# Sigmoid attention with mixture of depths: score units on other PSUM banks, one transpose a step earlier, and a last product in two halves

## The chip, the cores and the metric

The kernel runs on one core of one Trainium2 chip. The metric is the device time of one execution in microseconds (us), the median of several runs. Everything is float32.

## The reference

Two stages, the second fed by the first. The attention has no softmax: each score goes through a sigmoid of its own. Then, for each of the 8 batches, a gate picks 128 of the 448 tokens, and only those go through a two-layer network and are changed.

```python
# q, k, v: (8 batches, 12 heads, 448 tokens, 64)
scores = matmul(q, k^T) / sqrt(64) - log(448)
attn_out = matmul(sigmoid(scores), v)                  # (8, 12, 448, 64)
x = attn_out.transpose(0, 2, 1, 3).reshape(8, 448, 768)

scores = einsum('bsd,d->bs', x, w_gate)                # one gate score per token
out = x.copy()
for b in range(8):
    top_idx = argpartition(-scores[b], 128)[:128]      # the 128 tokens with the best scores
    xe = x[b, top_idx]
    ye = maximum(xe @ w1, 0) @ w2                      # w1: 768 x 1024, w2: 1024 x 768
    out[b, top_idx] = x[b, top_idx] + sigmoid(scores[b, top_idx])[:, None] * ye
```

## The kernel before: the parts concerned

The attention runs in 12 **steps** (s = 0 to 11), each for 8 heads. A step has 7 **units** (n = 0 to 6). A unit computes scores on TensorE into two PSUM tiles of two banks each, and ScalarE then takes each tile through the sigmoid into SBUF. `values` multiplies these with V; it comes in four parts, the first after the last unit of the step itself, the other three after units 0, 1 and 2 of the next step. So after units 3, 4 and 5 there is room on TensorE for the second stage: that is the table `WORK`.

All 8 PSUM banks are in use: the ring `psc` has two tiles, and the tiles `o0` and `o1` are single. Each tile has two banks. Tiles are given out again as soon as their last reader is done, so the reader decides when the next writer may start.

```python
def banks(which):
    if which == "any":                     # turn about: psc, o, psc, o ...
        turns[1] ^= 1
        which = "psc" if turns[1] else "o"
    if which == "psc":
        return ps_sc.tile([P, 2, 512], F32, name="psc")        # bufs=2
    if which == "o":
        turns[0] ^= 1                      # turn about: o0, o1
        which = turns[0]
    return ps_o[which].tile([P, 2, 512], F32, name=f"o{which}")  # bufs=1 each

def unit(s, n):
    if (s == 0 and n in (1, 3, 5)) or (s in (1, 2, 3) and n == NF + 1):   # NF = 3
        psc = [banks(0), banks(1)]
    else:
        psc = [banks("psc"), banks("psc")]
    ...                                    # 16 matmuls; heads 0, 1 into the first tile, 2, 3 into the second
    for pr in range(2):
        ...
        nc.scalar.activation(a, psc[pr][:, :, :S], AF.Sigmoid, bias=bias_s, scale=QK_SCALE)

def keep_busy(s):
    open_outs(s)                           # o0 and o1 for the coming values
    for _ in range(4):
        nc.tensor.matmul(outs[s][0][:, 0, :HP * TT], iden,
                         wg_b.rearrange("p h t -> p (h t)"), start=True, stop=True)
```

The result of `keep_busy` is used by nothing. When the fourth part of `values` is done, `take` moves `o0` and `o1` into the tokens-by-features layout with four VectorE transposes; then `gates` (multiply by the gate vector, add up) and `gate` (the scores of a whole batch, small operations, and a write to DRAM) follow on VectorE. `turn` is VectorE's transposing of q and k for a coming step. `ranking` finds each token's place among the scores (8 large VectorE operations and their followers), `choose` turns this into indices with small matmuls, and `fetch` has the chosen rows gathered from DRAM.

The second stage treats two batches at a time, a pair p. `("t", b)` is `turn_rows(b)`, which transposes the gathered rows of batch b on TensorE. The two layers are each done with 7 products in place of 8 blocks, from sums and differences of the blocks: `(1, p, key)` is a product of the first layer, `(2, p, key)` of the second, key 1 to 7.

```python
def turn_rows(b, where="o"):
    ...                                    # 6 transposes on TensorE into one tile
    if not odd:
        nc.scalar.activation(x[:, 0:2, :, :n], ps[:, :, :KH, :n], AF.Copy)
    else:
        nc.scalar.activation(x[:, 2, :, :n], ps[:, 0, :KH, :n], AF.Copy)
        nc.vector.tensor_copy(x[:, 3, :, :n], ps[:, 1, :KH, :n])
    ...
    for dst, y, z in ((4, 2, 0), (5, 3, 4), (2, 3, 2)):        # only after the odd batch
        nc.vector.tensor_tensor(out=x[:, dst, :, :n], in0=x[:, y, :, :n],
                                in1=x[:, z, :, :n], op=ALU.subtract)
    ...

ROWS1 = {1: 0, 2: 1, 3: 3, 4: 1, 5: 4, 6: 5, 7: 2}   # which x a product of the first layer reads
# after a product: key 1: ScalarE copy.  key 2: VectorE add, ScalarE relu.  key 6: VectorE add. ...
QUARTERS = {1: ((0, 0), (0, 1), (1, 0), (1, 1)), 2: ((0, 0),), 3: ((0, 1),), 4: ((1, 0),), ...}
# second layer: one VectorE operation per quarter adds the product to the gathered rows

WORK = {
    ...
    (7, 3): [(2, 0, 3)], (7, 4): [(2, 0, 6)], (7, 5): [(2, 0, 7), ("t", 2)],
    (8, 3): [("t", 3), (1, 1, 1)], (8, 4): [(1, 1, 2), (1, 1, 6)],
    ...
    (10, 3): [(2, 1, 3)], (10, 4): [(2, 1, 5), (2, 1, 6)], (10, 5): [(2, 1, 7)],
    (11, 3): [("t", 4)], (11, 4): [("t", 5), (1, 2, 1)], (11, 5): [(1, 2, 2)],
}
```

After step 11 comes `rest`: the last three parts of `values`, then all that is left of pairs 2 and 3. Work is issued in the order of the text, and each engine takes its instructions in this order.

```python
def rest():
    for n in range(3):
        gap(NS, n)                         # the last parts of values
    ...
    shared = banks("any")
    chosen = choose(b - 1, shared[:, 1])   # b = 7, p = 2
    work = [((1, p, 6), first(p, 6, ps=shared[:, 0])),
            ((1, p, 7), begin((1, p, 7), "any"))]
    gates(2 * NS - 1)
    fetch(*chosen)
    ...
    gate(waiting.pop())                    # the scores of batch 7
    spread(b, nc.sync)                     # and their way back from DRAM to all partitions
    ...
    for item, args in work:
        finish(item, args)
    for key in (4, 5):
        do((1, p, key), "any")
    first_sums(*begin((1, p, 3), "any"), sums_too=(5, 6))
    work = {key: begin((2, p, key), "any") for key in (2, 1, 4)}
    ranking(b)
    tile5 = banks("any")
    work[5] = second(p, 5, ps=tile5[:, 0])
    chosen = choose(b, tile5[:, 1])
    second_sums(*work[2])
    hidden_sum(p, 7)
    work[6] = begin((2, p, 6), "any")
    fetch(*chosen)
    second_sums(*work[1])
    ...
    for key in (1, 2, 6, 5, 3, 7, 4):      # pair 3, second layer: the end of the kernel
        do((2, p, key), "any")
```

Of the kernel before, what the change touches and what calls it, by code (L numbers as in the profile page):

```python
# [12 lines left out]
ALU = mybir.AluOpType  # L13
# [4 lines left out]
def kernel(  # L18
# [18 lines left out]
    TT = 32  # L37
# [251 lines left out]
    def unit(s, n):  # L289


        if (s == 0 and n in (1, 3, 5)) or (s in (1, 2, 3) and n == NF + 1):
            psc = [banks(0), banks(1)]
        else:
            psc = [banks("psc"), banks("psc")]
        if n == NF:
            parts = [(x, HK) for x in range(2)]
        else:
            x, c = divmod(n, NF + 1)
            parts = [(x, 4 * c), (x, 4 * c + 2)]  # L300
        for e in range(2):
            for y, (x, r) in enumerate(parts):
                for h in range(4):
                    d = slice(h * TT, (h + 1) * TT)
                    nc.tensor.matmul(  # L305
                        psc[h // 2][y * Dh:(y + 1) * Dh, h % 2, :S],
                        kT[2 * s + x][d, e, r:r + 2, :].rearrange("d r t -> d (r t)"),
                        qT[2 * s + x][d, e].rearrange("d r t -> d (r t)"),
                        start=(e == 0), stop=(e == 1))
        for pr in range(2):  # L310
            a = attn_tile(pr, f"d{s % 2}{n}" if n < 3 else f"u{n}")
            attn[s, pr, n] = a
            nc.scalar.activation(a, psc[pr][:, :, :S], AF.Sigmoid, bias=bias_s, scale=QK_SCALE)  # L313
# [3 lines left out]
    def open_outs(s):  # L317
        if s not in outs:
            outs[s] = [banks(0), banks(1)]

    def keep_busy(s):


        open_outs(s)
        for _ in range(4):
            nc.tensor.matmul(outs[s][0][:, 0, :HP * TT], iden,  # L326
                             wg_b.rearrange("p h t -> p (h t)"), start=True, stop=True)

    def values(s, n):

# [286 lines left out]
    def second_sums(p, key, ps):  # L617
        n = CAP
        left = pairs[p].setdefault("left", [6, 8])
        for x, m in QUARTERS[key]:  # L620
# [7 lines left out]
            if not left[x]:  # L628
                scatter(b)

    def scatter(b):
        n = CAP
        nc.gpsimd.indirect_dma_start(
# [19 lines left out]
    }  # L653

    LENT = {5: [(1, 6), (1, 7), (1, 5)], 6: [(1, 3), (2, 4), (2, 5)], 7: [(2, 6), (2, 7)],
# [63 lines left out]
    def gap(s, n):  # L719
# [23 lines left out]
        if n == 3 and s > 0 and not turned_next(s) and s != LATE:  # L743
            if waiting:
                gate(waiting.pop())
            gates(2 * s - 1)
            if waiting:
                gate(waiting.pop())

    def rest():  # L750
# [5 lines left out]
        for key, slot in (((2, 6), "d10"), ((2, 7), "d11")):  # L756
            lend(*key, slot)
        shared = banks("any")
        chosen = choose(b - 1, shared[:, 1])
        work = [((1, p, 6), first(p, 6, ps=shared[:, 0])),  # L760
                ((1, p, 7), begin((1, p, 7), "any"))]
        gates(2 * NS - 1)
        fetch(*chosen)

# [3 lines left out]
        store(b, (2, 3))  # L768
        for item, args in work:
            finish(item, args)  # L770
        for key in (4, 5):
            do((1, p, key), "any")
        first_sums(*begin((1, p, 3), "any"), sums_too=(5, 6))
        work = {key: begin((2, p, key), "any") for key in (2, 1, 4)}
        ranking(b)
        tile5 = banks("any")
        work[5] = second(p, 5, ps=tile5[:, 0])
        chosen = choose(b, tile5[:, 1])
        second_sums(*work[2])
        hidden_sum(p, 7)  # L780
        work[6] = begin((2, p, 6), "any")
        fetch(*chosen)
        second_sums(*work[1])
        hidden_sum(p, 3)
        work[7] = begin((2, p, 7), "any")
        for key in (4, 5, 6, 7):
# [11 lines left out]
            do((1, p, key), "any")  # L798
        for m in (5, 6, 7, 3):
            hidden_sum(p, m)  # L800
        for key in (1, 2, 6, 5, 3, 7, 4):
            do((2, p, key), "any")

    def stream():
        for b in range(B):
            routed(b)
        put(LATE, NU - 1.5, gates, 2 * LATE - 1)
        load(0)
        load(1)
        load(2)  # L810
# [9 lines left out]
        for s in range(NS):  # L820
            for n in range(NU):
# [9 lines left out]
                        for key in ((1, 3), (2, 4)):  # L831
                            lend(*key, "raw")
                gap(s, n)
                if n == NU - 2 and s in (1, 2, 3):
                    keep_busy(s)
                if n == NU - 2:
                    turn(2 * s + 2)
                    load(2 * s + 4)
# [43 lines left out]
```

## Time and profile before

| what | value |
|---|---|
| time, median of 3 runs | 457.12 us (456.84 to 457.91) |
| span of the profiled execution | 453.4 us |
| mean granted TensorE clock | 0.996 of full speed |
| scores: TensorE, into `psc` | 148.2 us busy, 2496 records, 540 ns each |
| scores: ScalarE, one sigmoid of 128x896 | 1.00 us each, 168 of them |
| `keep_busy` on TensorE | 4.7 us busy, 24 records |
| one product of the first layer, on the chain | 2.68 us |
| one product of the second layer, on the chain | 2.58 us |

Many of TensorE's records overlap, since matmuls on 32 rows run beside each other. So the length of one record says little. What counts is how far the chain of waits moves on while a group runs: a unit takes 1.50 us there when nothing holds it. A float32 matmul shows as two records.

### The profile page before, as it was taken

To read this page: it belongs to the slowest core of one execution; us is meant where nothing else is said; L and a number is where in the kernel's file an instruction comes from. 1 tells how busy PE (TensorE), PEld (TensorE's weight loads), DVE (VectorE), ACT (ScalarE), POOL (GpSimd) and SP (SyncE) were. 2 spreads that over 40 slices of the span, in tenths; PEclk is the share of its full clock that TensorE was granted. 3 is DMA by queue.
4 is the path that set the end of the run, shared out by engine and by line. 5 is a ranking of instruction groups with operands and counts; after the bars stand their busy time and mean duration, and the time that the engine had idled before them with its cause. 6 is when DMAs were issued, how large, how long until landed. Compare 5 with 4: busy or idle time off the path is not lost.

```text
span 453.4 us, 14452 instructions
## 1 busy us (share of the span) xinstructions
PE 442.0 (97%) x6398; PEld 267.0 (59%) x6398; DVE 303.8 (67%) x663; ACT 181.8 (40%) x237; POOL 32.5 (7%) x55
## 2 busy tenths in 40 slices
PE   8999999999999999999999999999999989999994
PEld 3474745565745845554445855654454639769952
DVE  4308679993844797887634697897742849994472
ACT  3856464555555254335444345334345520101100
POOL 7000000010000100000100000010010000001001
PEclk9999999999999999999999999999999999999998
DMA  8898898999866995995566883994833999811001
GB/s 279 214 329 193 329 342 187 267 205 319 175 201 220 139 234 192 170 233 186 117 235 174 132 222 142 193 196 159 241 106 101 259 189 267 147 37 71 1 0 69
DMA packets 128334, 84.67 MB, mean 187 GB/s; under 512 B 97600, under 2 KB 112064, under 8 KB 128272
## 3 DMA queue, kind: packets, MB, share of 16 engines
q1 hardware_dynamic: 126288, 75.84, 65.1%
q0 software_dynamic: 1984, 7.91, 5.7%
q8 instruction: 50, 0.82, 0.8%
q14 instruction: 12, 0.10, 0.1%
HBM read 63.28 MB, written 20.46 MB: 185 GB/s over the span
## 4 chain that ended last, share of the span: by engine, by line
PE 93%; DVE 3%; issue 1%; ACT 1%; DMA 1%; POOLq 0%; DVEq 0%; ACTq 0%
PE o L353 28%; PE psc L305 27%; PE o L548 13%; PE o L613 12%; PE psc L548 4%; PE psc L613 3%; PE o L305 3%; PE o L818 1%; PE o L326 1%; DVE x_b L368 1%; DMA out_dram<-xe,idx 1%; ACT attn_u L313 1%; DVE gate_p L379 1%; DVE scr L376 1%; PE o L467 0%
## 5 line engine op out<-in xcount | busy, mean ns | idle before, releaser
L305 PE MATMUL psc<-qT,kT 32*64 32x448 f32 x2496 | 148.2, 540 | 0.9 <-ACT attn_u L313 0.9
L313 ACT ACTIVATE attn_u<-psc,bias_s 128x896 f32<-128x896 f32 x86 | 81.9, 1004 | 84.4 <-PE psc L305 84.3
L353 PE MATMUL o<-attn_d,raw_v 32*64 32x448 f32 x960 | 104.5, 535 | 0.4 <-ACT o L356 0.4
L353 PE MATMUL o<-attn_u,raw_v 32*64 32x448 f32 x960 | 102.2, 535 | 0.8 <-ACT o L356 0.8
L305 PEld LDWEIGHTS psc<-qT,kT 32*64 32x64 f32 x2496 | 60.2, 131 | 59.1 <-issue 40.3
L313 ACT ACTIVATE attn_d<-psc,bias_s 128x896 f32<-128x896 f32 x70 | 66.7, 1003 | 46.5 <-PE psc L305 46.4
L368 DVE STREAM_TRANSPOSE x_b<-o 128x448 f32<-128x448 f32 x48 | 26.9, 618 | 66.6 <-PE o L353 59.3
L353 PEld LDWEIGHTS o<-attn_u,raw_v 32*64 32x64 f32 x960 | 41.2, 132 | 24.9 <-issue 19.9
L353 PEld LDWEIGHTS o<-attn_d,raw_v 32*64 32x64 f32 x960 | 40.4, 132 | 19.9 <-issue 17.3
L548 PEld LDWEIGHTS o<-rows_t,w_sb 128*128 128x128 f32 x264 | 30.4, 192 | 4.5 <-issue 1.4
L548 PEld LDWEIGHTS o<-rows_t,attn_d 128*128 128x128 f32 x264 | 30.3, 192 | 3.9 <-DVE scr L376 1.4
L548 PE MATMUL o<-rows_t,w_sb 128*128 128x128 f32 x264 | 31.9, 278 | 0.4 <-DVE rows_t L515 0.3
L548 PE MATMUL o<-rows_t,attn_d 128*128 128x128 f32 x264 | 31.6, 277 | 0.3 <-DVE rows_t L521 0.3
L379 DVE TENSOR_REDUCE gate_p<-scr 128x14 f32<-128x448 f32 x48 | 29.8, 622 | 1.7
L376 DVE TENSOR_TENSOR scr<-x_b,wg_b 128x448 f32<-128x448 f32 x48 | 29.6, 616 | 1.0
L624 DVE SCALAR_TENSOR_TENSOR xe<-o,gate,xe 128x384 f32<-128x384 f32 x37 | 21.1, 611 | 13.4 <-PE o L613 13.3
L280 DVE STREAM_TRANSPOSE kT<-raw_k 128x384 f32<-128x384 f32 x46 | 23.5, 548 | 6.9 <-PE psc L305 3.6
L613 PE MATMUL o<-attn_d,hidden 128*128 128x384 f32 x80 | 27.7, 494 | 0.0
L564 ACT ACTIVATE hidden<-hidden 128x512 f32<-128x512 f32 x12 | 7.5, 630 | 48.1 <-DVE hidden L561 48.1
L424 DVE TENSOR_SCALAR_CACHE_REDUCE scr<-rep,who 128x448 f32<-128x448 f32 (+1 forms) x32 | 21.5, 671 | 7.2 <-DMA rep<-scores 6.2
L613 PE MATMUL o<-w_sb,hidden 128*128 128x384 f32 x72 | 24.7, 491 | 0.0
L561 DVE TENSOR_TENSOR hidden<-o,hidden 128x512 f32<-128x512 f32 x24 | 16.0, 686 | 12.0 <-PE o L548 11.8
(117 smaller groups left out, 478.3 us busy)
## 6 DMA issues: line engine op xcount, KB each, us to landing
attn_d<-sum SPq DMA_DIRECT2D x42, 384.0 KB
out_dram<-x_b SPq DMA_DIRECT2D x32, 336.0 KB
raw_k<-in_k_dram SPq DMA_DIRECT2D x23, 448.0 KB
raw_q<-in_q_dram SPq DMA_DIRECT2D x23, 448.0 KB
raw_v<-in_v_dram SPq DMA_DIRECT2D x40, 192.0 KB
w_sb<-in_moe_w_dram SPq DMA_DIRECT2D x6, 768.0 KB
sum<-hidden SPq DMA_DIRECT2D x6, 768.0 KB
rep<-scores POOLq DMA_DIRECT2D x7, 224.0 KB, 5.3
```

The lines of the kernel that those rows point to most:

```text
L280: nc.vector.transpose(kT[i][:, e, :HK], sk[:, e, :HK].rearrange("p (m c) d -> p c m d", c=NF))
L305: nc.tensor.matmul(psc[h // 2][y * Dh:(y + 1) * Dh, h % 2, :S], kT[2 * s + x][d, e, r:r + 2, :].rearrange("d r t -> d (r t)"), qT[2 * s + ...
L313: nc.scalar.activation(a, psc[pr][:, :, :S], AF.Sigmoid, bias=bias_s, scale=QK_SCALE)
L353: nc.tensor.matmul(o[x][j * Dh:(j + 1) * Dh, pr, :S], w, a[rows, j, :], start=(n == 0 and c == 0), stop=(n == 3 and c == NF - 1))
L368: nc.vector.transpose(x_tiles[b][:, :, 2 * g + pr, :], outs[s][x][:, pr, :S].rearrange("p (r t) -> p r t", t=TT))
L376: nc.vector.tensor_tensor(out=tmp, in0=x_tiles[b][:, :, hp, :], in1=wg_b[:, hp:hp + 1, :].to_broadcast([P, TB, TT]), op=ALU.mult)
L379: nc.vector.tensor_reduce(out=gate_parts[b][:, :, hp], in_=tmp, axis=AX.X, op=ALU.add)
L424: nc.vector.tensor_scalar(out=junk[:n], in0=rep[:n], scalar1=own, scalar2=0.0, op0=ALU.is_gt, op1=ALU.add, accum_out=above[:n, c:c + 1])
L548: nc.tensor.matmul(ps[:, f, :n], w((t * FH + f) * P, P), x[:, t, :n], start=(t == 0), stop=(t == KH - 1))
L561: nc.vector.tensor_tensor(out=dst, in0=a, in1=b, op=ALU.add)
L613: nc.tensor.matmul(ps[:n, :DH], h[:, t, :n], w(t * DH, DH), start=(t == 0), stop=(t == FH - 1))
L624: nc.vector.scalar_tensor_tensor(out=xe[:n, cols], in0=ps[:n, :DH], scalar=st[b]["gate"][:n, 0:1], in1=xe[:n, cols], op0=ALU.mult, op1=ALU ...
```

## The change

**Other banks in steps 1 to 3.** The unit that uses `o0` and `o1` for its scores is now unit 5 (`NF + 2`), not unit 4 (`NF + 1`). The matmuls of `keep_busy` are gone. In step 2 the second `gates` comes after the `turn` for step 3, no longer ahead of it. This is to let the units go on without the filling matmuls.

**Turned rows at the end of step 10.** `("t", 4)` moves from step 11 to the end of the gap after unit 5 of step 10. The products of pair 2 in step 11 move up, and a third one, `(1, 2, 6)`, joins them; so `rest` begins with one product less, and its order and banks are adapted. This is to fill TensorE in step 11 and to shorten what follows.

**The last product in two halves of its columns.** Each half has a PSUM tile and a VectorE addition of its own, so that the addition of the first half can run beside the matmuls of the second.

```diff
@@ unit
-        if (s == 0 and n in (1, 3, 5)) or (s in (1, 2, 3) and n == NF + 1):
+        if (s == 0 and n in (1, 3, 5)) or (s in (1, 2, 3) and n == NF + 2):
@@ keep_busy and its call
-    def keep_busy(s):
-        ...
-                if n == NU - 2 and s in (1, 2, 3):
-                    keep_busy(s)
@@ new
+    def last_product(p, key):
+        n, w = CAP, DH // 2
+        h, wt = pairs[p]["h"][:, ROWS2[key]], weight(2, key, p)
+        (x, m), b = QUARTERS[key][0], 2 * p + QUARTERS[key][0][0]
+        xe = st[b]["xe"]
+        for y in range(2):
+            ps = bank("any")
+            cols = slice(m * DH + y * w, m * DH + (y + 1) * w)
+            for t in range(FH):
+                nc.tensor.matmul(ps[:n, :w], h[:, t, :n], wt(t * DH + y * w, w),
+                                 start=(t == 0), stop=(t == FH - 1))
+            nc.vector.scalar_tensor_tensor(
+                out=xe[:n, cols], in0=ps[:n, :w], scalar=st[b]["gate"][:n, 0:1],
+                in1=xe[:n, cols], op0=ALU.mult, op1=ALU.add)
+        pairs[p]["left"][x] -= 1
+        scatter(b)
@@ WORK
-        (10, 3): [(2, 1, 3)], (10, 4): [(2, 1, 5), (2, 1, 6)], (10, 5): [(2, 1, 7)],
-        (11, 3): [("t", 4)], (11, 4): [("t", 5), (1, 2, 1)], (11, 5): [(1, 2, 2)],
+        (10, 3): [(2, 1, 3)], (10, 4): [(2, 1, 5), (2, 1, 6)], (10, 5): [(2, 1, 7), ("t", 4)],
+        (11, 3): [(1, 2, 1)], (11, 4): [("t", 5), (1, 2, 2)], (11, 5): [(1, 2, 6)],
@@ gap: the second gates of step 2 (FIRST - 1 = 2) ...
-            gates(2 * s - 1)
+            if s != FIRST - 1:
+                gates(2 * s - 1)
@@ ... now after the turn
-        put(LATE, NU - 1.5, gates, 2 * LATE - 1)
+
+        for s in (FIRST - 1, LATE):
+            put(s, NU - 1.5, gates, 2 * s - 1)
@@ rest, pair 2
-        work = [((1, p, 6), first(p, 6, ps=shared[:, 0])),
-                ((1, p, 7), begin((1, p, 7), "any"))]
+        work = [((1, p, 7), first(p, 7, ps=shared[:, 0])),
+                ((1, p, 4), begin((1, p, 4), "any"))]
...
-        for key in (4, 5):
-            do((1, p, key), "any")
+        do((1, p, 5), "any")
...
-        work = {key: begin((2, p, key), "any") for key in (2, 1, 4)}
+        work = {key: begin((2, p, key), "any") for key in (1, 2, 4)}
...
-        second_sums(*work[2])
+        second_sums(*work[1])
...
-        second_sums(*work[1])
+        second_sums(*work[2])
@@ rest, pair 3
-        for key in (1, 2, 6, 5, 3, 7, 4):
+        for key in (1, 2, 6, 5, 3, 7):
             do((2, p, key), "any")
+        last_product(p, 4)
```

More of the change, by code (lines that the diff above doesn't have):

```diff
@@ L319, in open_outs @@
             outs[s] = [banks(0), banks(1)]
-    def keep_busy(s):
[L324 to L327, printed above, removed]
     def values(s, n):
```

## The prediction

> **What bounds the kernel now.** I read the page first, then the chain of waits, then the timelines of single engines around each place that the diff touches.
>
> ```profile
> PE 442.0 (97%) x6398; PEld 267.0 (59%) x6398; DVE 303.8 (67%) x663; ACT 181.8 (40%) x237; POOL 32.5 (7%) x55
> PE 93%; DVE 3%; issue 1%; ACT 1%; DMA 1%; POOLq 0%; DVEq 0%; ACTq 0%
> ```
>
> TensorE looks full, and 93% of the chain lies on it. But its records overlap and stretch over waits, so the change has to be read from the places where TensorE stands on someone else. There are three kinds.
>
> First, step 1, units 4 to 6 and the filling matmuls (L326) on TensorE, then ScalarE beside them:
>
> ```profile
> 36.24 2.35 PE L305 MATMUL o<-qT,kT 32*64 32x448 f32 x26
> 40.40 1.57 PE L326 MATMUL o<-wg_b,iden 128*128 128x192 f32 x8
> 41.89 2.25 PE L305 MATMUL psc<-qT,kT 32*64 32x448 f32 x26
> ```
>
> ```profile
> 36.31 1.91 ACT L313 ACTIVATE attn_u<-psc,bias_s 128x896 f32<-128x896 f32 x2 [1.88 <-PE psc L305]
> 39.01 1.91 ACT L313 ACTIVATE attn_u<-o,bias_s 128x896 f32<-128x896 f32 x2 [0.80 <-PE o L305]
> 40.81 1.91 ACT L313 ACTIVATE attn_u<-psc,bias_s 128x896 f32<-128x896 f32 x2
> ```
>
> A unit costs TensorE 1.50 us, its pair of sigmoids costs ScalarE 1.91, and each unit on `psc` waits for the sigmoids of the last unit on `psc`. So here ScalarE sets the pace, and L326 only fills the wait for the sigmoids that end at 42.72. After a second tile comes free, the unit waiting for it ends 1.80 us later: 42.72 to 44.52, and in unit 4, 37.15 (last transpose out of `o1`) to 38.96.
>
> Second, VectorE in steps 2 and 3. From 59.77 (the transposes of step 2) to 102.7 its timeline has no gap over 0.15 us. At the end of step 3 it decides when step 4 begins:
>
> ```profile
> 96.22 1.07 DVE L287 STREAM_TRANSPOSE qT<-raw_q 128x896 f32<-128x896 f32 x1
> ```
>
> ```profile
> 97.41 1.06 PEld L305 LDWEIGHTS psc<-qT,kT 32*64 32x64 f32 x32 [0.44 <-issue]
> ```
>
> The transpose of q ends at 97.29, and the 32 weight loads of the first unit come in one burst at 97.41: they were waiting.
>
> Third, the end: `choose` for batch 7 in `rest`, VectorE and then the chain:
>
> ```profile
> 392.94 0.68 DVE L424 TENSOR_SCALAR_CACHE_REDUCE scr<-rep,who 128x448 f32<-128x448 f32 x1 [0.37 <-DMA rep<-scores]
> 398.93 0.69 DVE L439 TENSOR_TENSOR hot<-slots,place_s 128x512 f32<-128x512 f32 x1
> ```
>
> ```profile
> 400.53 0.79 PE psc L467 x8
> ```
>
> The ranking starts when the scores come back from DRAM, ends at 399.62, and `choose` runs at 400.53. There is 0.9 us of slack and no more.
>
> [...] in step 11 the VectorE copy out of the transposed rows (L515) starts at 358.02, right behind the gate work queued ahead of it, though ScalarE's copy out of the same tile, which it follows, had ended at 355.53. [...] the granted clock here is 1.00 in every 2 us stretch from 34 to 46 us,[...] so I charge nothing.
>
> **Part 1, steps 1 to 3.** By step 1's own times. Unit 3's sigmoids end at 37.27 and 38.22. Unit 4, now on `psc`, waits for the second and ends at 38.22 + 1.81 = 40.03; before 38.96. Its sigmoids end at 41.03 and 41.98. Unit 5 finds `o0`, `o1` long free, ends at 41.53; sigmoids 41.98 to 43.89. Unit 6 waits for 41.98 and ends at 43.79, not 44.52. But `values` writes to `o0`, `o1`, which unit 5's sigmoids hold until 43.89. Of its 64 records 8 are through by then; the other 56 take 56/8 x 0.375 (eight weight loads per 0.375 us in the timeline) plus 0.5 to start: 47.0. Before: 44.52 + 3.0 = 47.5. So 0.5 us saved in step 1. Taking out L326 saves nothing: it lay in the wait.
>
> The same working gives 0.5 in step 2 and 1.0 in step 3 for TensorE, but there VectorE is full, and its work until the q of step 4 is the same in sum (moving `gates` behind `turn` only changes the order). It starts 0.5 earlier thanks to step 1, and the wait of its index operation for `choose` (86.9 to 87.04) goes. So step 4 begins about 0.6 earlier. **-0.6 us.**
>
> **Part 2a, step 10.** The kernel before has the new arrangement elsewhere: step 7 ends with a product, a turn and a `choose`. The chain there, and in step 10:
>
> ```profile
> 221.25 2.79 PE o L613 x8
> 224.07 1.15 DVE xe L624 x2
> 225.26 0.61 PE o L463 x4
> 225.87 1.69 PE psc L305 x32
> ```
>
> ```profile
> 328.04 2.78 PE o L613 x8
> 330.82 0.34 PE o L463 x4
> 331.15 1.69 PE psc L305 x32
> ```
>
> With a turn in between, `choose` gets the tile of the product just done and waits for its two additions. From the end of the product to the end of unit 6: 3.52 us with the turn, 2.02 without. **+1.5**, of which 0.66 is the turn itself, moved from step 11.
>
> **Part 2b, step 11**, times as before (+1.5 at the end). TensorE, ScalarE and VectorE before:
>
> ```profile
> 350.55 2.65 PE L305 MATMUL psc<-qT,kT 32*64 32x448 f32 x32 [0.33 <-ACT attn_u L313]
> 358.63 2.94 PE L548 MATMUL o<-rows_t,w_sb 128*128 128x128 f32 x24 [0.26 <-DVE rows_t L515]
> ```
>
> ```profile
> 358.02 0.55 DVE L515 COPY rows_t<-o 128x384 f32<-128x384 f32 x1
> 358.49 1.61 DVE L521 TENSOR_TENSOR rows_t<-rows_t 128x384 f32<-128x384 f32 x3
> ```
>
> Waits before: 1.4 us at unit 4 and 0.3 at L515. After: unit 3 ends at 349.4; product 1 to 352.2; unit 4 no longer waits, 353.9; turn 354.5; product 2 to 357.2; unit 5 to 358.9. Product 6 reads the second difference of L521, ready at 359.6: a wait of 0.6, and it ends at 362.5. So far well filled. But product 2 now comes ahead of unit 5, so its relu stands ahead of unit 5's sigmoids in ScalarE's queue. It waits for VectorE: L521 to 360.1, L531 0.56, the addition 0.68, so 361.3; relu 0.63, to 361.95. Unit 5's sigmoids, whose scores are there at 358.9, run 361.95 to 363.86. Unit 6 needs their tiles: 363.86 + 1.81 = 365.7, against 363.26 before. **+2.4** in step 11, with one product of 2.68 done in advance.
>
> **Part 2c, rest.** Counted from the end of `values` (375.72 before). TensorE before: `choose` 0.98, five products of the first layer, four of the second: 24.7. Now one less: 22.1. But the ranking's end hangs on VectorE, DRAM and VectorE, which nothing shortens: 399.62 - 375.72 = 23.9. So `choose` waits 1.8 us and ends at 24.9. Then product (2,2,6) takes the `psc` tile of product 1, whose four additions come behind the ranking in VectorE's queue: 23.9 + 4 x 0.545 = 26.1. It begins at about 26.2; before at 401.32 - 375.72 = 25.6. From there both are alike. **+0.6**: the whole saved product is lost in two waits.
>
> **Part 3, the tail.** Two halves take as long as one product: L326's loads of 192 columns come 0.154 us apart, (1.27 - 0.19)/7, against 2.58/8 = 0.32 for 384 columns. The last addition now has 192 columns; from 0.35 us for 128 and 0.61 for 384 I estimate 0.42. **-0.2.**
>
> Sum: -0.6 + 1.5 + 2.4 + 0.6 - 0.2 = +3.7. 457.12 + 3.7 = **460.8 us**.
>
> **Rivals.** (A) The parts do what they are for: steps 1 to 3 gain 2.0 since VectorE isn't the limit, and step 11 and `rest` gain the removed waits. Then some 455. For: TensorE is 93% of the chain. Against: VectorE has no gap to give from 59.8 to 102.7, and the slack at `choose` is 0.9. (B) The relu doesn't hold the sigmoids, as VectorE is done sooner; step 11 costs 1.0, the total is 459.4. For: in step 8, with the same order, the relu is out of the way at 254.5, and the sigmoids wait for nobody. Against: there the gates of the whole batch come later in VectorE's queue. (C) Without filling, the clock falls in steps 1 to 3;[...] 463 to 466. Against: waits before the change of 1.4 us left the clock at 1.00.
>
> **Range and chances.** Step 10 is measured elsewhere in the same trace; step 11 and `rest` are each good to about 1 us, part 1 to about 1 us, mostly to the fast side. 8 in 10: 458.2 to 462.8. 2% is 9.1 us, far from anything worked out here: faster 0.01, within 0.97, slower 0.02.
>
> **What would show it.** Step 4 begins 0.6 us earlier with q's transpose still last; `choose` of step 10 waits on VectorE (L616 in the new numbering) for some 0.5 us; a hole in ScalarE's sigmoids of step 11 that ends with the relu; `choose` of batch 7 waiting on VectorE's `hot`, and the next product on the additions. I am wrong if the sigmoids of unit 5 in step 11 start right behind its matmuls, or if the ranking of batch 7 ends much sooner than 23.9 us after `values`.

## The result, and the profile after

The changed kernel takes **463.37 us** (median of 4 runs, 462.74 to 463.85), the kernel before, run beside it, 457.51 us (456.84 to 458.10). The ratio is 1.0128, 95% interval 1.0106 to 1.0149: slower, by 5.9 us. The prediction had 460.8 and a range up to 462.8, so it missed by 2.6 us, in the right direction. The two profiled executions lie further apart, 453.4 and 461.7 us of span, since the one of the kernel before was a short one (its device time was 455.25 us).

The head of the page of the changed kernel:

```profile
PE 444.1 (96%) x6382; PEld 274.0 (59%) x6382; DVE 303.8 (66%) x664; ACT 182.1 (39%) x237; POOL 33.8 (7%) x55
PE 72%; DVE 15%; DMA 7%; issue 3%; ACT 1%; POOLq 0%; DVEq 0%; SPq 0%; ACTq 0%
```

TensorE carried 93% of the chain before and 72% now. VectorE has 15% and DMA 7%: the chain of waits runs through them, above all in four places. (Lines of the changed kernel from L345 on are those of the kernel before 8 lower: L345, L540, L605, L616 for L353, L548, L613, L624.)

*First,* the ranking of batch 0, in the chain of waits of steps 2 and 3 (start, length, what):

```profile
66.59 7.51 DMA scores<-total
74.68 3.77 DMA rep<-scores
78.47 0.70 DVE scr L416 x2
```

In the trace of the kernel before no DMA stands on the chain here. The way of the scores through DRAM takes 11.9 us in this execution, and VectorE stands 0.84 us for them. The change is not needed for such a wait: in the traces of `e1_only_turn` and `e3_only_tail` below, whose steps 1 to 3 are those of the kernel before, VectorE stands 0.46 and 0.39 us at the same place. At the end of step 3 q's transpose still comes last, as in the prediction, but at 97.97, not 97.29. This is VectorE's timeline, and then TensorE's weight loads:

```profile
96.90 1.07 DVE L287 STREAM_TRANSPOSE qT<-raw_q 128x896 f32<-128x896 f32 x1
```

```profile
98.08 0.27 PEld L305 LDWEIGHTS psc<-qT,kT 32*64 32x64 f32 x16 [1.02 <-PE o L345]
```

*Second,* the end of step 10, in the chain of waits:

```profile
329.68 2.79 PE o L605 x8
332.49 1.15 DVE xe L616 x2
333.69 0.61 PE o L455 x4
334.30 1.69 PE psc L305 x32
```

From the start of the product to the end of unit 6 it is 335.98 - 329.68 = 6.30 us; before, 332.84 - 328.04 = 4.80. The two additions stand between the product and `choose`, as in step 7 before.

*Third,* step 11. ScalarE's timeline in the kernel before, where the relu (L564) comes behind unit 5's sigmoids, and in the changed kernel (the bracket is the idle time before, and what ended it):

```profile
358.44 1.91 ACT L313 ACTIVATE attn_u<-psc,bias_s 128x896 f32<-128x896 f32 x2 [1.13 <-PE psc L305]
362.80 0.63 ACT L564 ACTIVATE hidden<-hidden 128x512 f32<-128x512 f32 x1 [2.46 <-DVE hidden L561]
```

```profile
357.24 1.91 ACT L313 ACTIVATE attn_u<-psc,bias_s 128x896 f32<-128x896 f32 x2 [1.13 <-PE psc L305]
359.03 0.49 ACT L506 ACTIVATE rows_t<-o 128x384 f32<-128x384 f32 x1
359.40 0.21 ACT L509 ACTIVATE gate<-got 128x1 f32<-128x1 f32 x1
364.33 0.63 ACT L556 ACTIVATE hidden<-hidden 128x512 f32<-128x512 f32 x1 [4.72 <-DVE hidden L553]
364.87 1.89 ACT L313 ACTIVATE attn_u<-psc,bias_s 128x896 f32<-128x896 f32 x2
```

ScalarE stands for 4.72 us in front of the relu (L556), which waits for VectorE. Unit 5's scores had been there since 362.3, but their sigmoids run behind it, at 364.87. From the end of unit 6 of step 10 to that of step 11 it is 32.58 us; before, 30.42.

*Fourth,* `rest`: TensorE's timeline, from the last product ahead of `choose` (L459) on.

```profile
401.93 1.45 PE L605 MATMUL o<-qT,hidden 128*128 128x384 f32 x4
404.55 1.05 PE L459 MATMUL o<-who,hot 128*128 128x2 f32 x8 [1.17 <-DVE hot L431]
406.66 5.49 PE L605 MATMUL psc<-attn_d,hidden 128*128 128x384 f32 x8 [1.05 <-DVE xe L616]
411.94 3.20 PE L605 MATMUL o<-attn_d,hidden 128*128 128x384 f32 x8
```

The two predicted waits are there, `choose` for `hot` and product 6 for the additions. They are about 1.1 us each. What was not predicted is the length of the two products behind them: on the chain 5.49 + 3.00 = 8.5 us, where the kernel before has 2.69 + 2.58 = 5.3:

```profile
401.32 2.69 PE o L613 x8
404.00 2.58 PE psc L613 x8
```

The table by stretches of the changed kernel shows why. The columns are the stretch, its length, busy time of TensorE, weight loads, VectorE, ScalarE, GpSimd, then the granted clock, the DMA share and GB/s:

```profile
404.50:405.50 1.00, 0.95 (x8) 0.95 (x8) 1.00 (x3) 0.00 (x0) 0.00 (x0) 1.00 0.03 8
405.50:406.50 1.00, 0.11 (x1) 0.02 (x1) 1.00 (x3) 0.00 (x0) 0.00 (x0) 0.76 0.00 0
406.50:407.50 1.00, 0.84 (x2) 0.54 (x3) 1.00 (x5) 0.00 (x0) 0.00 (x0) 0.50 0.00 0
...
411.50:412.50 1.00, 1.00 (x3) 0.47 (x2) 0.32 (x1) 0.00 (x0) 0.00 (x0) 0.50 0.08 31
412.50:413.50 1.00, 1.00 (x4) 0.66 (x3) 1.00 (x3) 0.00 (x0) 0.00 (x0) 0.82 0.00 0
```

The clock fell to 0.50 at about 406.0 and came back at 412.85: 6.8 us at half speed.

**Where the 8.3 us between the two traces lie.** Before step 10's product +1.64; step 10 +1.50; step 11 +2.16; its values +0.02; `rest` up to product 6 0.0; the two products +3.2; after them 0.0; the tail -0.26. Of the 1.64, 0.48 is already there when the first matmuls end, and 0.15 comes by step 4. The other 1.0 lies in work that the change leaves as it was: 0.2 in step 6, 0.4 in step 9, where a ranking waits for its scores from DRAM (12.5 us), and 0.4 at the start of step 10. The causes of the first and the last of these were not found.

Steps 10 and 11 themselves vary little between executions. Steps 9 to 11 take 99.0 us in all four traces that have the old `WORK` (the kernel before and three runs below), and step 11 takes 32.57 to 32.59 us in the nine that have the new one there as it is. Most of the scatter sits in steps 1 to 4: 105.6 us in the trace of the kernel before, the shortest of all, and up to 111.0 in the others.

### The profile page after: what moved, and what is told of

It reads as the page before. It is cut to its first block, busy times and chain, and to the rows that moved or that the text cites. A ratio compares the mean times of both kernels' runs of the same rounds, so it can differ in the third digit from the quotient of the medians.

```text
span 461.7 us, 14427 instructions
## 1 busy us (share of the span) xinstructions
PE 444.1 (96%) x6382; PEld 274.0 (59%) x6382; DVE 303.8 (66%) x664; ACT 182.1 (39%) x237; POOL 33.8 (7%) x55
## 4 chain that ended last, share of the span: by engine, by line
PE 72%; DVE 15%; DMA 7%; issue 3%; ACT 1%; POOLq 0%; DVEq 0%; SPq 0%; ACTq 0%
PE o L345 22%; PE psc L305 21%; PE o L605 11%; PE o L540 9%; DMA scores<-total 3%; DMA rep<-scores 3%; PE psc L605 3%; PE psc L540 2%; DVE x_b L360 2%; DVE scr L368 2%; DVE scr L419 2%; DVE scr L416 2%; DVE gate_p L371 2%; PE o L305 1%; PE o L832 1%
## 5 line engine op out<-in xcount | busy, mean ns | idle before, releaser
L305 PE MATMUL psc<-qT,kT 32*64 32x448 f32 x2496 | 152.5, 543 | 3.3 <-ACT attn_u L313 2.9
L345 PE MATMUL o<-attn_d,raw_v 32*64 32x448 f32 x960 | 107.2, 536 | 0.3 <-ACT o L348 0.3
L345 PE MATMUL o<-attn_u,raw_v 32*64 32x448 f32 x960 | 105.0, 535 | 0.8 <-ACT o L348 0.8
L305 PEld LDWEIGHTS psc<-qT,kT 32*64 32x64 f32 x2496 | 63.6, 131 | 61.4 <-issue 34.1
L345 PEld LDWEIGHTS o<-attn_u,raw_v 32*64 32x64 f32 x960 | 43.7, 132 | 22.2 <-issue 14.2
L345 PEld LDWEIGHTS o<-attn_d,raw_v 32*64 32x64 f32 x960 | 41.4, 132 | 18.9 <-issue 14.6
L540 PEld LDWEIGHTS o<-rows_t,attn_d 128*128 128x128 f32 x264 | 30.2, 192 | 5.1 <-issue 2.0
L540 PE MATMUL o<-rows_t,attn_d 128*128 128x128 f32 x264 | 31.7, 277 | 0.8 <-issue 0.5
L616 DVE SCALAR_TENSOR_TENSOR xe<-o,gate,xe 128x384 f32<-128x384 f32 x36 | 20.5, 611 | 14.3 <-PE o L605 14.3
L605 PE MATMUL o<-attn_d,hidden 128*128 128x384 f32 x80 | 28.1, 499 | 0.0
L540 PEld LDWEIGHTS o<-rows_t,w_sb 128*128 128x128 f32 x216 | 24.8, 192 | 4.0 <-issue 1.4
L556 ACT ACTIVATE hidden<-hidden 128x512 f32<-128x512 f32 x12 | 7.5, 630 | 49.6 <-DVE hidden L553 49.6
L540 PE MATMUL o<-rows_t,w_sb 128*128 128x128 f32 x216 | 26.2, 278 | 0.2 <-DVE x_b L360 0.2
L605 PE MATMUL o<-w_sb,hidden 128*128 128x384 f32 x72 | 24.7, 491 | 0.4 <-DVE x_b L360 0.4
L553 DVE TENSOR_TENSOR hidden<-o,hidden 128x512 f32<-128x512 f32 x25 | 16.7, 687 | 12.8 <-PE o L540 12.5
```

The source lines that it names most:

```text
L305: nc.tensor.matmul(psc[h // 2][y * Dh:(y + 1) * Dh, h % 2, :S], kT[2 * s + x][d, e, r:r + 2, :].rearrange("d r t -> d (r t)"), qT[2 * s + ...
L345: nc.tensor.matmul(o[x][j * Dh:(j + 1) * Dh, pr, :S], w, a[rows, j, :], start=(n == 0 and c == 0), stop=(n == 3 and c == NF - 1))
L540: nc.tensor.matmul(ps[:, f, :n], w((t * FH + f) * P, P), x[:, t, :n], start=(t == 0), stop=(t == KH - 1))
L553: nc.vector.tensor_tensor(out=dst, in0=a, in1=b, op=ALU.add)
L605: nc.tensor.matmul(ps[:n, :DH], h[:, t, :n], w(t * DH, DH), start=(t == 0), stop=(t == FH - 1))
L616: nc.vector.scalar_tensor_tensor(out=xe[:n, cols], in0=ps[:n, :DH], scalar=st[b]["gate"][:n, 0:1], in1=xe[:n, cols], op0=ALU.mult, op1=ALU ...
```

## The experiments

The theory after the comparison, **C**: beside the waits of steps 10 and 11 that the prediction had, the holes of about 1 us in `rest` make the clock fall. Its rival **W** / **N**: the slow products are waiting for something, or are an accident of one trace. Ratios are to the kernel before on the same chip, with the 95% interval. Kernels of one group below shared a chip.

### Each part alone

`e1_only_turn`: the kernel before with the second part only, that is the new `WORK` for steps 10 and 11 and the new order of `rest`, as in the diff of the change.

> The kernel before with part 2 alone (the turn at the end of step 10, the three products in step 11, the new order in rest). Theory C (clock): the two waits around the choose of batch 7 leave TensorE so thin that its granted clock halves, and the product after them takes 5.5 us, not 2.6. Then this part alone costs 1.5 + 2.2 + 3.2 = about +6.5 us, and the clock in rest shows 0.5 for some 6 us. Rival Q (queues only): what my prediction named, +4.0 to +4.5 us, clock 1.00 in rest; the rest of the loss then comes from steps 1 to 3.

`e2_only_banks`: the first part only.

```diff
-(s in (1, 2, 3) and n == NF + 1)
+(s in (1, 2, 3) and n == NF + 2)
-                if n == NU - 2 and s in (1, 2, 3):
-                    keep_busy(s)
+            if s != FIRST - 1:
                 gates(2 * s - 1)
-        put(LATE, NU - 1.5, gates, 2 * LATE - 1)
+        for s in (FIRST - 1, LATE):
+            put(s, NU - 1.5, gates, 2 * s - 1)
```

> The kernel before with part 1 alone (unit 5 on the other banks, no filling matmuls, the gates of step 2 behind the turn). The prediction had -0.6 us. Theory D (DRAM): the ranking of batch 0 cannot start before its scores come back from DRAM, some 12 us after they were written, so step 4 starts no earlier: 0 us, between -0.4 and +0.4. Rival F (filling): without the filling matmuls the clock falls at the end of step 3 (0.5 for 4 us) and that costs +1 us or more.

`e3_only_tail`: the third part only (`last_product` in place of the last `do`).

> The kernel before with part 3 alone (the last product in two halves). Both theories: -0.2 us, too small to tell from 0 by the times; in the trace the last VectorE operation takes some 0.42 us and not 0.62, and from the end of the addition of product 3 to the end of the span it is about 0.2 us less than the 11.2 us of before.

`e4_no_fill`: the kernel before without `keep_busy`, nothing else.

```diff
-                if n == NU - 2 and s in (1, 2, 3):
-                    keep_busy(s)
```

> The kernel before without the 12 filling matmuls of steps 1 to 3, nothing else changed. The prediction: they lie in the wait for the sigmoids of unit 5, so 0 us (within 0.4). Rival F (filling): TensorE is idle for 2.3 us in each of the three steps, the clock halves in one or more of them, and the time rises by 1 to 5 us.

Measured, beside 457.05 us of the kernel before:

| kernel | median us | ratio | 95% interval |
|---|---|---|---|
| `e1_only_turn` | 461.89 | 1.0100 | 1.0060 to 1.0141 |
| `e2_only_banks` | 457.45 | 1.0012 | 0.9988 to 1.0037 |
| `e3_only_tail` | 456.93 | 0.9984 | 0.9965 to 1.0003 |
| `e4_no_fill` | 457.92 | 1.0014 | 0.9985 to 1.0043 |

The loss is the second part's. The other two are nothing that can be told from zero. Rival C of the prediction, a loss by the missing filling in steps 1 to 3, falls: without it the clock is 1.00 from 30 to 100 us in the traces of `e2_only_banks` and `e4_no_fill`. The changed kernel's own trace has 3.4 us of 0.50 at 88.6, in step 3, but so has `e3_only_tail`, at 89.9, which keeps the filling. `e16_step11_filled` below, which also keeps it, has the same at 90.2. Over all runs there is a hint of an effect: the mean clock was 0.995 or less in 7 of 14 runs of `e4_no_fill`, in 8 of 43 of the kernel before, and in none of 14 of `e2_only_banks`. This would fit a use of the filling with the old banks, which the new banks make needless; but no trace shows it, and in time neither shows.

The trace of `e2_only_banks` shows what became of part 1. Its first matmuls end at 6.37 us (6.39 before) and unit 0 of step 2 at 48.55 (49.03): the gain of step 1 is there. But VectorE then stands 1.29 us until the scores of batch 0 are back, and unit 0 of step 4 ends at 99.84 (99.25). That is the run's theory D.

The trace of `e1_only_turn` shows the losses of steps 10 and 11 again, at 1.5 us and with the relu ahead of unit 5's sigmoids. But product 6 in `rest`, on TensorE's timeline, is short, and the clock stays at 1.00:

```profile
403.21 1.05 PE L467 MATMUL o<-who,hot 128*128 128x2 f32 x8 [0.26 <-DVE hot L439]
405.31 2.85 PE L613 MATMUL psc<-attn_d,hidden 128*128 128x384 f32 x8 [1.05 <-DVE xe L624]
```

Its wait at `choose` was 0.26 us, not 1.17. That execution took 459.6, the shortest of its runs (up to 463.44). Taken alone, this trace and the +4.6 us by the ratio fit rival Q of the run's expectation (+4.0 to +4.5, clock at 1.00) better than theory C (+6.5); but the mean clock was 0.995 or less in 4 of the 6 runs. So the clock must be judged over many runs.

### Each suspected loss taken away

All four are the changed kernel with one edit. `e5_rest_fill`, seven matmuls whose result nothing uses:

```diff
+        for _ in range(7):
+            nc.tensor.matmul(tile5[:, 1, :HP * TT], iden,
+                             wg_b.rearrange("p h t -> p (h t)"), start=True, stop=True)
         chosen = choose(b, tile5[:, 1])
```

> The changed kernel with seven idle matmuls of 192 columns put ahead of the choose of batch 7, in the place where TensorE waits for the ranking. Theory C (the granted clock falls to 0.50 because TensorE is thin for about 3 us there, and the next two products then take 8.5 us in place of 5.3): the clock is 1.00 from the choose to the end of the second-layer products in rest, these two products take 5.3 us on the chain, and the time is 3.2 us less than that of the changed kernel in runs where the clock fell, about 460.5 (3.5 us above the kernel before), with a spread of 2 us. Theory W (the two products are slow because they wait for their inputs or weights, not for the clock): they still take over 8 us, and the time stays at 463.4 or a little more.

`e6_six_first`:

```diff
+        second_sums(*work[1])
         ranking(b)
         tile5 = banks("any")
         work[5] = second(p, 5, ps=tile5[:, 0])
+        work[6] = begin((2, p, 6), "any")
         chosen = choose(b, tile5[:, 1])
-        second_sums(*work[1])
         hidden_sum(p, 7)
-        work[6] = begin((2, p, 6), "any")
```

> The changed kernel with the two additions of product 1 issued ahead of the ranking, and product 6 of pair 2's second layer ahead of the choose of batch 7, so that real work lies in the wait. Theory C (wait and clock): both the 2.6 us of the saved product and the 3.2 us of the clock come back, choose ends 24.9 us after the last values, the clock is 1.00 there, and the time is 457.6 (about equal to the kernel before). Theory W (no clock, waits alone): 2.6 us come back, 460.8. Theory V (VectorE and the way through DRAM decide when the last gathered rows come, whatever TensorE does meanwhile): no more than 1 us comes back, 462.5.

`e7_relu_late`, where `b` begins a product and `f` does its addition and relu:

```diff
-(11, 4): [("t", 5), (1, 2, 2)], (11, 5): [(1, 2, 6)],
+(11, 4): [("t", 5), ("b", 1, 2, 2)], (11, 5): [("f", 1, 2, 2), (1, 2, 6)],
```

> The changed kernel with the sum and the relu of product 2 of pair 2 issued after the sigmoids of unit 5 in step 11; the product itself stays where it is. Theory R (in step 11 the loss is the relu ahead of the sigmoids in ScalarE's queue): unit 5's sigmoids start right behind its matmuls, and step 11 from its start to the end of unit 6 is 1.4 us shorter than in the changed kernel (31.2 in place of 32.6), time 462.0. Rival T (the loss is TensorE's own extra product and its waits for VectorE's differences): step 11 stays at 32.6, time 463.4.

`e8_turn_first`:

```diff
-(10, 5): [(2, 1, 7), ("t", 4)],
+(10, 5): [("t", 4), (2, 1, 7)],
```

> The changed kernel with the turn of batch 4 in step 10 ahead of product 7, so that choose in step 10 no longer gets the tile of the product just done. Theory B (0.84 of the 1.5 us are choose waiting for the two additions on that tile, and 0.66 the turn itself): step 10 from the start of the product or turn to the end of unit 6 is 5.5 us in place of 6.3, and no VectorE additions stand on the chain there; time 462.5. Rival T (the turn itself and its copies cost it all): 6.3 as before, time 463.4.

Measured, beside 458.57 us of the kernel before: `e5_rest_fill` 461.29 (ratio 1.0083, 1.0051 to 1.0116), `e6_six_first` 459.98 (1.0037, 1.0019 to 1.0054), `e7_relu_late` 462.63 (1.0081, 1.0048 to 1.0114), `e8_turn_first` 463.63 (1.0097, 1.0063 to 1.0130). The intervals of the last two hold the changed kernel's ratio or nearly, so here the traces decide.

TensorE's timeline of `e5_rest_fill`: the idle matmuls (L790) fill the hole, no wait is left, the clock is 1.00 throughout, and product 6 takes its normal time.

```profile
403.10 2.44 PE L790 MATMUL o<-wg_b,iden 128*128 128x192 f32 x14
405.38 0.95 PE L459 MATMUL o<-who,hot 128*128 128x2 f32 x8
406.19 2.83 PE L605 MATMUL psc<-attn_d,hidden 128*128 128x384 f32 x8
```

From the end of the values of step 11 to the end of the two products it is 30.8 us here, 34.1 in the changed kernel, 30.9 in the kernel before. So W falls: the products wait for nothing but the clock. Nor do the idle matmuls let product 6 start sooner: it begins 25.5 us after the values here, 24.8 to 25.6 in the six traces without filling or work in the hole. In `e6_six_first` the same stretch is 29.6 us: real work in the hole gains 1.3 on the kernel before, half of the saved product, where its theory C had all of it.

`e7_relu_late`, ScalarE's timeline:

```profile
362.45 1.91 ACT L313 ACTIVATE attn_u<-psc,bias_s 128x896 f32<-128x896 f32 x2 [2.79 <-PE psc L305]
364.38 0.63 ACT L556 ACTIVATE hidden<-hidden 128x512 f32<-128x512 f32 x1
```

Unit 5's sigmoids start when its scores are there (362.45), and the relu comes behind them. Step 11 is 31.49 us, 1.09 less than 32.58: theory R holds, somewhat smaller than the 1.4 expected. TensorE still stands 0.53 us ahead of product 6, as in the changed kernel.

`e8_turn_first`, the chain of waits of step 10:

```profile
332.45 0.81 PE o L501 x6
333.26 2.58 PE o L605 x8
335.84 0.54 PE o L455 x4
336.38 1.69 PE psc L305 x32
```

No addition is left on the chain; 5.62 us in place of 6.30. The order inside one gap was worth 0.68.

Both of these still have a slow product 6 in `rest`, 4.40 and 4.34 us, with the clock at 0.50 for 3.4 us each.

### The clock, with the kernels on one chip

`e9_after_again` is the changed kernel unaltered.

> The changed kernel once more, unaltered, for its spread and for a second trace. Theory C (the clock falls in the hole ahead of the choose of batch 7 and stays low for a multiple of about 3.4 us, seen so far as 3.4 and 6.8): the hole from the end of the last first-come second-layer product to the start of product 6 is 2.4 to 3.2 us, the clock then is 0.50 for 3.4 or 6.8 us, and the time is 4.5 to 7 us above the kernel before. Rival (the low clock of the first trace was an accident): clock 1.00 there, and the time 3.6 above the kernel before.

It took 462.21 us beside 458.93 (ratio 1.0081, 1.0045 to 1.0117), less than in the first measurement and near the 3.6 us that the rival had. But the clock fell again, for 3.4 us; TensorE's timeline:

```profile
404.36 1.05 PE L459 MATMUL o<-who,hot 128*128 128x2 f32 x8 [0.86 <-DVE hot L431]
406.47 4.24 PE L605 MATMUL psc<-attn_d,hidden 128*128 128x384 f32 x8 [1.05 <-DVE xe L616]
```

With this the filled kernel (1.0083) and the changed kernel were equal by ratio, though on two chips. So they were run together:

> The changed kernel, on one chip with the filled ones. Theory C: mean clock below 0.996 in most runs, a stretch of 3.4 or 6.8 us at 0.50 behind the wait in rest, and a time 1.5 to 3.5 us above the kernel with idle matmuls there. Theory N (the clock in rest is an accident of single traces): the same time as that kernel, within 0.7 us.

> The changed kernel with seven idle matmuls in the wait ahead of the choose of batch 7. Theory C: 1.5 to 3.5 us below the changed kernel of the same call, 2.5 to 4 above the kernel before, mean clock 0.996 or more in most runs. Theory N: the time of the changed kernel, within 0.7 us.

> The changed kernel with product 6 of pair 2's second layer in the wait, ahead of the choose of batch 7. Theory C with the wait: as the kernel with idle matmuls, and 1.2 us less (rest took 29.6 us up to the end of the product before the turn there, 30.8 with idle matmuls), so 3 to 4.5 us below the changed kernel of the same call. Theory N: 1.2 below the changed kernel.

| kernel (beside 458.78 us) | median us | ratio | 95% interval | median of the runs' clocks |
|---|---|---|---|---|
| `e13_after_third` | 463.27 | 1.0090 | 1.0059 to 1.0121 | 0.993 |
| `e14_fill_again` | 461.28 | 1.0054 | 1.0035 to 1.0073 | 0.997 |
| `e15_six_again` | 460.18 | 1.0034 | 1.0017 to 1.0051 | 0.998 |

Idle matmuls that compute nothing make the kernel 2.0 us faster at the median, and real work in their place another 1.1. The 2.0 is not known well: the intervals of the first two ratios overlap a little. The traces have 4.24 + 2.58 = 6.82 us for the two products with 3.4 us of low clock (`e9_after_again`) and 2.85 + 2.58 = 5.43 without (`e13_after_third`), so one such stretch costs 1.4 us there, and the 6.8 us of the first trace cost 3.2. The clocks decide whether there is an effect: over all executions of the changed kernel the mean granted clock was 0.995 or less in 17 of 23, over those of the four filled runs (`e5`, `e6`, `e14`, `e15`) in 8 of 63. N falls.

The profiled execution of `e13_after_third` itself had no fall. Its TensorE timeline, cut at 412, the clock being 1.00 and product 6 2.85 us on the chain:

```profile
406.63 1.45 PE L605 MATMUL o<-qT,hidden 128*128 128x384 f32 x4
408.69 1.05 PE L459 MATMUL o<-who,hot 128*128 128x2 f32 x8 [0.60 <-DVE hot L431]
410.79 1.56 PE L605 MATMUL psc<-attn_d,hidden 128*128 128x384 f32 x4 [1.05 <-DVE xe L616]
```

Here are the six traces with the hole unfilled and the order of `choose` as in the changed kernel, from the end of the last product to the start of product 6: 3.28 us (`after`, fell for 6.8), 3.08 (`e7`, 3.4), 2.97 (`e9`, 3.4), 2.71 (`e13`, none), 2.60 (`e8`, 3.4), 2.36 (`e1`, none). About 1 us of each is `choose`. The hole's length follows the scores' way through DRAM, which took 7.11 us in `after`, 6.92 in `e7`, 6.80 in `e9`, 6.54 in `e13` and 6.45 in `e8`.

That the clock fell with a hole of 2.60 us and not with one of 2.71 was not explained. In `after` it fell at 88.58 and at 406.02; between them lie 317.44 us, 93 times 3.413. In `e8` it fell at 76.62 and at 407.71, 331.1 us or 97 times 3.413 apart. Here are the 3.41 us ahead of the second fall in each of the two, with the columns as in the table by stretches:

```profile
402.61:406.02 3.41, 1.83 (x11) 1.13 (x9) 3.31 (x10) 0.00 (x0) 0.00 (x0) 1.00 0.01 3
404.30:407.71 3.41, 2.23 (x12) 1.35 (x10) 3.33 (x8) 0.00 (x0) 0.00 (x0) 1.00 0.01 2
```

TensorE's busy time there includes `choose`. Without it, 2.64 us of the first stretch and 2.23 of the second hold no matmul. But the hole of `e13`, from 408.08 to 410.79, is 2.71 us without a matmul other than those of `choose`, and the clock stayed at 1.00; and the first fall in `e8`, at 76.62, came behind 3.41 us of which only 1.52 held no matmul. So these lengths alone do not tell whether the clock falls; what does stays open.

### Versions meant to beat the kernel before

`e10_all_mended`: the changed kernel with the edits of `e6`, `e7` and `e8`, and `second_sums(*work[2])` ahead of `hidden_sum(p, 7)`.

> The changed kernel with all mendings at once: turn of batch 4 ahead of product 7 in step 10, the relu of product 2 behind unit 5's sigmoids in step 11, product 6 ahead of the choose of batch 7 in rest, and product 2's addition right after the ranking. If the losses add up as the single runs showed them: step 10 +0.8 against the kernel before, step 11 +1.1, rest -2.0, tail -0.2, so 0.3 us below the kernel before, clock 1.00 in rest. If they do not add up (VectorE or DRAM decides in rest): 1 us or more above it.

457.23 us beside 458.93: ratio 0.9978, 0.9959 to 0.9998. Step 10 took 5.60 us, +0.8 as expected, and `rest` up to the product ahead of the turn 28.8, -2.1; the clock is 1.00 there. Step 11 took 32.0, +1.6 in place of +1.1. With -0.2 for the tail these make +0.1, so the trace does not show the 1.0 us by which the time is lower.

`e11_product_later` fills step 11 from the other side: no turn moves, and product 3 of pair 1 goes from step 10 to step 11.

```diff
-(10, 3): [(2, 1, 3)], (10, 4): [(2, 1, 5), (2, 1, 6)], (10, 5): [(2, 1, 7)],
-(11, 3): [("t", 4)],
+(10, 3): [(2, 1, 5)], (10, 4): [(2, 1, 6)], (10, 5): [(2, 1, 7)],
+(11, 3): [("t", 4), (2, 1, 3)],
```

> The kernel before, its steps 1 to 3 and rest untouched, with the last product in two halves and another way to fill step 11: no turn moved; product 3 of pair 1 goes from step 10 (where unit 4 had two products behind it) to step 11, behind the turn of batch 4. Theory H (step 11 lacks work behind unit 3, so TensorE waits 1.4 us at unit 4): step 10 gets one product, 2.58 us, shorter, step 11 only 1.2 to 1.8 us longer, and the time is 1.0 below the kernel before. Rival R (the relu and VectorE's queue decide when unit 6's sigmoids run, as in the changed kernel): what is gained at unit 4 is lost there, and the time is that of the kernel before.

`e12_product_later_relu` has `("b", 1, 2, 2)` at `(11, 5)` and `("f", 1, 2, 2)` at `(11, 6)` on top.

> As the run before it, and the addition and relu of product 2 of pair 2 issued after unit 6's sigmoids in step 11. Theory H with R (both count): 1.6 below the kernel before. If the relu did not stand in the way: 1.0 below, as the run before it. If VectorE's late addition holds a tile that the values need: at or above the kernel before.

They took 457.79 (0.9974, 0.9954 to 0.9994) and 457.99 (0.9987, 0.9965 to 1.0009), beside 458.93. So the relu does not matter here; step 11 is 32.5 us in both traces. In `e11_product_later` step 10 became 1.7 us shorter and step 11 2.1 longer, so by its trace the gain in time is not that of theory H. A wait came up that nobody expected; TensorE's timeline in step 10:

```profile
320.97 2.82 PE L613 MATMUL o<-attn_d,hidden 128*128 128x384 f32 x8 [0.90 <-DMA attn_d<-sum]
```

Product 5, now the first of the step, finds its weights not yet loaded: unit 3 had ended at 320.07, they land at 320.83, and TensorE stands for 0.90 us. So in the next one a product with weights that are always in SBUF stands there:

```diff
-(9, 3): [(2, 1, 1), (2, 1, 2)],
-(10, 3): [(2, 1, 3)],
-(11, 3): [("t", 4)],
+(9, 3): [(2, 1, 1)],
+(10, 3): [(2, 1, 2)],
+(11, 3): [(2, 1, 3), ("t", 4)],
```

> The kernel before, its steps 1 to 3 and rest untouched, last product in two halves; product 2 of pair 1 goes from step 9 to step 10, product 3 from step 10 to step 11, ahead of the turn of batch 4 there, so that every product finds its weights loaded and TensorE has work behind unit 3 of step 11. Theory H (TensorE's wait of 1.4 us at unit 4 of step 11 is all that is filled): step 9 is 2.6 us shorter, step 11 only 1.2 longer, and the time 1.6 below the kernel before, with step 10 as it was. Rival V (the added work shifts VectorE's queue, and the products of step 11 wait for its differences instead): step 11 is 2.2 or more longer, and the time 0.6 below the kernel before or equal to it.

`e16_step11_filled` took 457.77 beside 458.78: ratio 0.9970, 0.9950 to 0.9989, the best of all, 1.4 us below the kernel before. Its chain of waits in step 11 holds TensorE alone:

```profile
352.06 1.50 PE psc L305 x30
353.57 2.82 PE o L613 x8
356.39 0.66 PE o L509 x6
357.05 1.69 PE psc L305 x32
```

Step 11 is 32.2 us, 1.8 more than before for 2.6 us of added work. The wait of 1.4 us at unit 4 is gone, but 0.7 is lost at the start of the step: the second part of the values begins 5.2 us into it, 4.5 before. It was so in `e10_all_mended` and `e11_product_later` too; what makes it longer was not found. Step 10, which should have stayed as it was, is 0.6 longer for the same reason, and step 9 is 2.1 shorter, not 2.6.

So where these versions gain is not shown. From the end of step 8 to the end of the program the traces have 189.1 us for the kernel before, 189.2 for `e10`, 189.3 for `e11`, 190.3 for `e12` and 189.2 for `e16`; what stands ahead of it is the same work as in the kernel before for `e11`, `e12` and `e16`. The ratios of `e10`, `e11` and `e16` lie below 1 with their intervals, but by time alone, and only just. Theories H and V of the last run stay undecided: by time 1.4 us are nearer to H (1.6) than to V (0.6), and the interval, 0.5 to 2.3, holds both; step 11 at +1.8 lies between them too.

## Why the prediction was wrong, point by point

- **Clock: "so I charge nothing".** This is the step that failed. I took single waits, and those in steps 1 to 3 only. In `rest` I had the two waits worked out, 1.8 and about 1.3 us, with `choose` between them, and didn't see that together they are one thin stretch: by the prediction's own numbers 22.1 to 26.2, or 4.1 us; 3.28 in the trace. The runs showed a clock of 0.50 there. It cost 2.0 us at the median on one chip (463.27 to 461.28), 3.2 in the profiled execution. Ahead of the last 9 us of each trace, the low stretches last 3.4 us seven times (`after` at 88.6, `e3` at 89.9, `e7` at 405.2, `e8` at 76.6 and 407.7, `e9` at 405.9, `e16` at 90.2) and 6.8 once (`after` at 406.0).
- **Part 1, -0.6.** The step-1 gain came as worked out: unit 0 of step 2 ended at 49.05, 49.03 before, though the first matmuls had ended 0.48 later. It was lost by step 4 (its first unit ended at 99.88, 99.25 before): the working took VectorE to be full there, but VectorE stood 0.84 us for scores that were not back from DRAM, and 1.29 in `e2_only_banks`. By time part 1 alone is 1.0012 (0.9988 to 1.0037), and rival A's gain of 2.0 in these steps falls. Whether -0.6 or 0 is right the runs cannot tell: over all traces steps 1 to 4 took 105.6 to 110.7 us in the old form (six traces) and 105.7 to 111.0 in the new (eleven).
- **Part 2a, +1.5.** Exact: 6.30 - 4.80. `e8_turn_first` splits it into 0.68 for the order and 0.82 for the turn, where the working had 0.84 and 0.66.
- **Part 2b, +2.4.** The mechanism was right, to the queue: the relu ended at 364.96, ScalarE's hole ends with it. Measured +2.16. Rival B (the relu doesn't hold the sigmoids, +1.0) falls; moving the relu brings step 11 to +1.07, about what B had for it.
- **Part 2c, +0.6.** Both waits came, and product 6 began 25.62 us after the values, 25.60 before: 0.0 in place of +0.6, as the additions began 0.5 sooner than worked out. That the saved product is lost in the waits was right: over the six traces with the hole, product 6 begins 0 to 0.8 us sooner than before, of 2.6 saved.
- **Part 3, -0.2.** -0.26 in the trace, and the last addition is 0.42 us, the estimate. By time 0.9984, not to be told from 0. The chain's last entries show what keeps it small: it ends with the scatter of the other batch, which starts ahead of both halves' additions:

```profile
450.73 0.63 DVE xe L616
451.36 0.27 issue
451.62 3.02 DMA out_dram<-xe,idx
```

- **The sum.** The other terms, as the trace has them, are 1.5 + 2.16 + 0.0 - 0.26 = +3.4 without part 1, near the predicted +3.7. The trace of `e13_after_third`, in which the clock did not fall, has +3.4 from the end of step 8 on as well. With 2.0 for the clock it is +5.4, against +5.9 in the first measurement and +3.7 and +4.1 in the repeats (0.0081 of 458.9 us and 0.0090 of 458.8). So the term that was left out accounts for most of the miss. But the first measurement lies at the upper end of three, and the intervals of the two repeats hold the predicted +3.7. If they are nearer the truth, the prediction's sum comes out right by luck, since about 2 us of it are the clock, which it did not charge; the runs do not settle more than a microsecond of it.

## What to carry to other kernels

Add up waits that stand close together: here two waits of 0.3 to 1.2 us with a few small matmuls between them cost TensorE's clock in four of six traces, a transfer through DRAM ahead of them made their length vary from run to run, and 2.60 us from end to end lost the clock in one trace where 2.71 left it at 1.00 in another. Moving work forward gains only if the place that it leaves has other work ready. Look there first for what ends the wait, and pull real work into it, as product 6 here. Before a product is moved across a unit, check three queues: whose additions hold the tile it gets, whose relu stands ahead of the sigmoids, and when its weights land.

## What was not expected of the hardware

- The clock fell to 0.50 where TensorE had been thin for only 2.6 to 3.3 us, of which `choose` was busy for 1, and stayed there for 3.4 us or twice that although TensorE was full again in less than 1 us.
- The scores' way through DRAM and back took 7.1 us in `rest`, 11.9 in step 2 and 12.5 in step 9 of one execution; it alone can put the ranking on the chain.
- The kernel before varies from 456.0 to 462.3 us on one chip. The clock is not the only cause of such scatter: the profiled run of `e14_fill_again` took 464.73 at a clock of 0.997. Its chain of waits in step 4 has, inside one unit, 1.97 us in which TensorE waited for nothing that the profile shows:

```profile
103.80 1.97 issue
```

The profiled run of `e13_after_third`, 464.89, has 2.52 at the same place. What it was stays open.
